# An MLP-mixer block: gelu in units of 2048 columns, and its cubic constant added to 64 columns

## The chip, the core and the metric

The kernel runs on one core of a Trainium2 chip. A core has TensorE (matrix products, called PE in the profile), VectorE (DVE), ScalarE (ACT), GpSimd (POOL) and SyncE (SP, which here starts transfers), and they run their own instruction queues side by side. The metric is the device time of one execution in microseconds; less is better.

## The reference

`x` has 2048 rows of 512 columns, `w1` and `w2` are 512x512, `w3` is 512x1792 and `w4` 1792x512, all bf16.

```python
def reference(x, w1, w2, w3, w4):
    B, S, D = x.shape
    h = _gelu(_layernorm(x, axis=-1) @ w1)
    c = D // 4
    # the four column quarters of h are shifted along the rows by 1, -1, 2 and -2
    g0 = jnp.pad(h[:, :, 0*c:1*c], ((0, 0), (1, 0), (0, 0)))[:, :S, :]
    ...  # g1, g2, g3 likewise
    hs = jnp.concatenate([g0, g1, g2, g3], axis=-1) @ w2
    x1 = x + hs
    h2 = _gelu(_layernorm(x1, axis=-1) @ w3) @ w4
    return x1 + h2
```

Gelu is the tanh approximation. With y its input it can be written y * sigmoid(C2 * y * (y*y + K)), where K = 1/0.044715 and C2 = 2 * sqrt(2/pi) * 0.044715. The kernel computes it so.

## The kernel before

The program builds a list of operations per engine with what each reads and writes, and a small scheduler merges the lists: it estimates each operation's time (the `dur` arguments) and fixes the order on each engine by those estimates. On the chip each engine then works through its own list in that order and waits on semaphores. The order of the instructions is therefore part of the program, and a change of a `dur` or of a buffer count can move it.

The stages: layernorm of `x` by VectorE (statistics, then normalization); transposition of the normalized rows by TensorE; first product (`L564` with `xnT`), gelu, the mixer product with `w2` (`L584`; `L580` adds `x`), which gives `x1`; then layernorm of `x1`, transposition by DMA (`L370`), second product (`L564` with `x1nT`), gelu, product with `w4` (`L602`), addition of `x1` (`L517`) and store.

The work on the hidden columns is cut into output blocks: 128 hidden columns (on the partitions) by 512 rows, one PSUM bank each. The first layer has 4 blocks for each of four stages of 512 rows, the second 14. Two blocks, 1024 columns in the free dimension, go through gelu together:

```python
GW = 1024
NYP = 3
NYSB = 4
NX2 = 3
NU = 3
NSG = 3
# ...
xnT = sb("xnT", [P, DC, S], BF16)
x1nT = sb("x1nT", [P, DC, S], BF16)
ysb = sb("ysb", [P, NYSB, GW], BF16)
x2b = sb("x2b", [P, NX2, GW], BF16)
ub = sb("ub", [P, NU, GW], BF16)
sgb = sb("sgb", [P, NSG, GW], BF16)
# ...
def add_c0(gb):
    ps = gb % NYP
    sc.add("act", f"c0_{gb}",
           lambda e: e.activation(ysb[:, gb % NYSB, :],
                                  y_ps[:, GW * ps : GW * (ps + 1)], ACT_F.Copy),
           reads=[(("y", (2 * gb) % NYB), 2 * gb), (("y", (2 * gb + 1) % NYB), 2 * gb + 1)],
           writes=[(("ysb", gb % NYSB), gb)], dur=1080)

def add_c1(gb, eng="dve"):
    y = ysb[:, gb % NYSB, :]
    if eng == "act":
        fn = lambda e: e.activation(x2b[:, gb % NX2, :], y, ACT_F.Square)
        dur = 1080
    else:
        fn = lambda e: e.tensor_tensor(x2b[:, gb % NX2, :], y, y, ALU.mult)
        dur = 640
    sc.add(eng, f"c1_{gb}", fn,
           reads=[(("ysb", gb % NYSB), gb)], writes=[(("x2", gb % NX2), 2 * gb)],
           dur=dur)

def add_c2a(gb):
    x2 = x2b[:, gb % NX2, :]
    sc.add("dve", f"c2a_{gb}",
           lambda e: e.tensor_scalar(x2, x2, GELU_K, None, ALU.add),
           reads=[(("x2", gb % NX2), 2 * gb)],
           writes=[(("x2", gb % NX2), 2 * gb + 1)], dur=450)

def add_c2b(gb):
    y = ysb[:, gb % NYSB, :]
    sc.add("dve", f"c2b_{gb}",
           lambda e: e.tensor_tensor(ub[:, gb % NU, :], x2b[:, gb % NX2, :], y, ALU.mult),
           reads=[(("ysb", gb % NYSB), gb), (("x2", gb % NX2), 2 * gb + 1)],
           writes=[(("u", gb % NU), gb)], dur=640)

def add_c3(gb):
    sc.add("act", f"c3_{gb}",
           lambda e: e.activation(sgb[:, gb % NSG, :], ub[:, gb % NU, :],
                                  ACT_F.Sigmoid, scale=GELU_C2),
           reads=[(("u", gb % NU), gb)], writes=[(("sg", gb % NSG), gb)], dur=1160)

def add_c4(gb, eng="dve"):
    layer, st, fc0 = blk_info(gb)
    y = ysb[:, gb % NYSB, :].rearrange("p (i s) -> p i s", i=2)
    sg = sgb[:, gb % NSG, :].rearrange("p (i s) -> p i s", i=2)
    rd = [(("ysb", gb % NYSB), gb), (("sg", gb % NSG), gb)]
    if layer == 2:
        dst = h2T[:, fc0 : fc0 + 2, st % 2, :]
        w = [(("h2T", j, st % 2, q), st) for j in (fc0, fc0 + 1) for q in range(4)]
        sc.add(eng, f"c4_{gb}", lambda e: e.tensor_tensor(dst, y, sg, ALU.mult),
               reads=rd, writes=w, dur=640)
        return
    # ... the first layer writes the same product to hT in one to four pieces (L503)
```

`add_c0` copies two PSUM banks to `ysb` (`L447`, ScalarE). VectorE then squares (`c1`, `L458`; the branch for ScalarE is not taken), adds K (`c2a`, `L467`) and multiplies by y (`c2b`, `L474`); ScalarE takes the sigmoid (`c3`, `L480`); VectorE multiplies y by it (`c4`, `L492` in the second layer). A buffer slot is free for its next writer when its last reader is done: a `ysb` slot after `c4`, a PSUM bank after `c0`. `h2T` holds two stages of 512 rows, so the third stage's `c4` waits until the first stage's `L602` products are done. The lists are made like this:

```python
def gelu_blocks(blocks):
    LAG = 1
    for i, gb in enumerate(blocks):
        add_c0(gb)
        add_c1(gb, c1_eng(gb))
        add_c2a(gb)
        add_c2b(gb)
        if i >= LAG:
            add_c3(blocks[i - LAG])
            add_c4(blocks[i - LAG])
    for gb in blocks[len(blocks) - LAG :]:
        add_c3(gb)
        add_c4(gb)
# ...
for st in range(NST):
    for fc in range(DC):
        add_ygroup(1, st, fc)
        tn = 4 * (st + 1) + fc
        if DEV["head_pe_tp"] and fc < 4 and tn < NT:
            g = st * DC + fc
            add_head_tp(tn, after=[(("y", g % NYB), g)])
gelu_blocks(list(range(NB1)))
# ... mixer products, second layernorm, second product (add_ygroup), gelu, w4 product (add_mm4)
```

`add_ygroup` is one output block, four matmuls of 128x128 by 128x512. `add_head_tp` transposes one tile of 128 normalized rows (four matmuls against the identity), and may run when the block named in `after` is done. `add_mm4` is one tile of 128 output rows: 14 matmuls into one of the two banks of `o_ps`, which VectorE empties (`L517`).

Of the kernel before, what the change touches and what calls it, by code (L numbers as in the profile page):

```python
# [6 lines left out]
P = 128  # L7
# [162 lines left out]
def bass_standalone__mixer_s_mlp__prompt_kernel(  # L170
# [19 lines left out]
    NYSB = 4  # L190
    NX2 = 3
    NU = 3
    NSG = 3
# [3 lines left out]
    BPS1 = DC // 2  # L197
    BPS2 = FC // 2
    NB1 = NST * BPS1
    NB2 = NST * BPS2  # L200
    NB = NB1 + NB2
    NG1 = NST * DC
    assert NG1 == 2 * NB1
# [4 lines left out]
    with ExitStack() as es:  # L208
# [4 lines left out]
        x1nT = sb("x1nT", [P, DC, S], BF16)  # L213
# [18 lines left out]
        ysb = sb("ysb", [P, NYSB, GW], BF16)  # L232
        x2b = sb("x2b", [P, NX2, GW], BF16)
        ub = sb("ub", [P, NU, GW], BF16)
        sgb = sb("sgb", [P, NSG, GW], BF16)
# [129 lines left out]
        def add_xT_dma(layer, t, eng="sp"):  # L365
            gt = q_ln(layer, t)
            dstT = xnT if layer == 1 else x1nT
            cb = t if layer == 1 else gt - NT
            sc.add(eng, f"dmaT{gt}",
                   lambda e: e.dma_start(dstT[:, :, P * cb : P * (cb + 1)],  # L370
                                         xn_buf[:, gt % NXN, :], transpose=True),
                   reads=[(("xn", gt % NXN), gt)], writes=[(("xT", layer, cb), 0)],
                   dur=1300, queue=eng)
# [61 lines left out]
        def blk_info(gb):  # L435
            if gb < NB1:
                st, fp = divmod(gb, BPS1)
                return 1, st, 2 * fp
            st2, fp = divmod(gb - NB1, BPS2)
            return 2, st2, 2 * fp  # L440

        NYB = 2 * NYP

        def add_c0(gb):
            ps = gb % NYP
            sc.add("act", f"c0_{gb}",
                   lambda e: e.activation(ysb[:, gb % NYSB, :],  # L447
                                          y_ps[:, GW * ps : GW * (ps + 1)], ACT_F.Copy),
                   reads=[(("y", (2 * gb) % NYB), 2 * gb), (("y", (2 * gb + 1) % NYB), 2 * gb + 1)],
                   writes=[(("ysb", gb % NYSB), gb)], dur=1080)  # L450

        def add_c1(gb, eng="dve"):
            y = ysb[:, gb % NYSB, :]
            if eng == "act":
                fn = lambda e: e.activation(x2b[:, gb % NX2, :], y, ACT_F.Square)
                dur = 1080
            else:
                fn = lambda e: e.tensor_tensor(x2b[:, gb % NX2, :], y, y, ALU.mult)  # L458
                dur = 640
            sc.add(eng, f"c1_{gb}", fn,  # L460
                   reads=[(("ysb", gb % NYSB), gb)], writes=[(("x2", gb % NX2), 2 * gb)],
                   dur=dur)

        def add_c2a(gb):
            x2 = x2b[:, gb % NX2, :]
            sc.add("dve", f"c2a_{gb}",
                   lambda e: e.tensor_scalar(x2, x2, GELU_K, None, ALU.add),  # L467
                   reads=[(("x2", gb % NX2), 2 * gb)],
                   writes=[(("x2", gb % NX2), 2 * gb + 1)], dur=450)

        def add_c2b(gb):
            y = ysb[:, gb % NYSB, :]
            sc.add("dve", f"c2b_{gb}",
                   lambda e: e.tensor_tensor(ub[:, gb % NU, :], x2b[:, gb % NX2, :], y, ALU.mult),  # L474
                   reads=[(("ysb", gb % NYSB), gb), (("x2", gb % NX2), 2 * gb + 1)],
                   writes=[(("u", gb % NU), gb)], dur=640)

        def add_c3(gb):
            sc.add("act", f"c3_{gb}",
                   lambda e: e.activation(sgb[:, gb % NSG, :], ub[:, gb % NU, :],  # L480
                                          ACT_F.Sigmoid, scale=GELU_C2),
                   reads=[(("u", gb % NU), gb)], writes=[(("sg", gb % NSG), gb)], dur=1160)

        def add_c4(gb, eng="dve"):
            layer, st, fc0 = blk_info(gb)
            y = ysb[:, gb % NYSB, :].rearrange("p (i s) -> p i s", i=2)
            sg = sgb[:, gb % NSG, :].rearrange("p (i s) -> p i s", i=2)
            rd = [(("ysb", gb % NYSB), gb), (("sg", gb % NSG), gb)]
            if layer == 2:
                dst = h2T[:, fc0 : fc0 + 2, st % 2, :]  # L490
                w = [(("h2T", j, st % 2, q), st) for j in (fc0, fc0 + 1) for q in range(4)]
                sc.add(eng, f"c4_{gb}", lambda e: e.tensor_tensor(dst, y, sg, ALU.mult),  # L492
                       reads=rd, writes=w, dur=640)
                return
            for si, (dst, spec, ng, ncols, w) in enumerate(c4_segments(fc0, st)):
                if ng == 2:
                    yy, ss = y, sg
                else:
                    gi, c0 = spec
                    yy = y[:, gi, c0 : c0 + ncols]  # L500
                    ss = sg[:, gi, c0 : c0 + ncols]
                sc.add(eng, f"c4_{gb}_{si}",
                       (lambda d_, a_, b_: (lambda e: e.tensor_tensor(d_, a_, b_, ALU.mult)))(dst, yy, ss),  # L503
                       reads=rd, writes=w, dur=60 + 0.57 * ncols * ng)
# [40 lines left out]
        def add_head_evac(t):  # L545
# [3 lines left out]
                   reads=res, writes=[(("xT", 1, t), 0)], dur=600)  # L549
# [285 lines left out]
```

## Time and profile before

| | |
|---|---|
| time, median of 5 | 161.35 us (161.01 to 162.32) |
| span of the profiled execution | 159.2 us |
| TensorE matmul busy | 138.3 us, 87% |
| VectorE busy | 127.7 us, 80% |
| ScalarE busy | 91.9 us, 58% |
| GpSimd busy | 18.9 us, 12% |
| granted TensorE clock | full throughout |

The span runs from the first instruction to the last of one profiled execution, whose time is listed as 161.01 us. A line of the profile names the line of the program, the engine, the operation and what it writes and reads; `x28` is the number of instructions. Busy time counts each engine's instructions where they overlap only once. In a listing in order of time, an instruction's length runs until its result is written, so neighbours on one engine overlap a little: the distance between starts is what an instruction costs in a full queue. An engine named behind an arrow is the one that ended a wait.

### The profile page before, as it was taken

The page shows a single profiled execution, that of the slowest core. Times are in us where ns is not written, and L with a number is a line of the kernel's source. Part 1 is how long each engine was busy: PE and PEld are TensorE (multiplying, and loading weights), DVE is VectorE, ACT ScalarE, POOL GpSimd, SP SyncE. Part 2 cuts the span into 40 slices and gives each one's busy share as a digit, 9 for nine tenths or more (in the row PEclk, how much of TensorE's full clock was granted, in tenths as well). Part 3 has the DMA queues.
Part 4 walks back from the last instruction along what each step waited for, and adds up shares of the span by engine and source line. Part 5 has one row for each costly group of instructions (what it writes and reads, how often), then busy time and mean ns, then how long its engine had stood idle before and what let it go on. Part 6 is the DMA issues. An engine that isn't in the chain of part 4 may idle for free.

```text
span 159.2 us, 1881 instructions
## 1 busy us (share of the span) xinstructions
PE 138.3 (87%) x656; PEld 60.8 (38%) x656; DVE 127.7 (80%) x268; ACT 91.9 (58%) x110; POOL 18.9 (12%) x46
## 2 busy tenths in 40 slices
PE   0079696798999899998899899999989999988992
PEld 0044232343444344443344344444434444433440
DVE  1799699999999999999999999559999139981311
ACT  3185568998955459787786875119885008520000
POOL 4022750020164441000000000000000000000000
PEclk9999999999999999999999999999999999999999
DMA  5930400057069844430000000010000001110010
GB/s 163 339 157 0 129 3 2 4 146 315 2 188 305 170 66 99 99 66 2 0 4 33 0 0 33 0 66 33 0 0 4 33 33 49 52 35 33 33 65 34
DMA packets 13432, 11.12 MB, mean 70 GB/s; under 512 B 9136, under 2 KB 12208, under 8 KB 13424
## 3 DMA queue, kind: packets, MB, share of 16 engines
q1 hardware_dynamic: 12016, 6.29, 15.0%
q0 software_dynamic: 880, 4.19, 8.0%
q10 hardware_dynamic: 528, 0.52, 1.0%
q8 instruction: 5, 0.08, 0.2%
q14 instruction: 3, 0.02, 0.1%
HBM read 6.82 MB, written 2.10 MB: 56 GB/s over the span
## 4 chain that ended last, share of the span: by engine, by line
PE 32%; DVE 27%; issue 3%; ACT 1%
PE o_ps L602 27%; DVE ub L474 7%; DVE h2T L492 6%; DVE x2b L458 6%; PE y_ps L564 6%; DVE x2b L467 4%; DVE o_sb L517 2%; ACT ysb L447 1%; DVE xn_buf L430 1%; DVE st L381 1%; DVE mv L386 0%; ACT sgb L480 0%
## 5 line engine op out<-in xcount | busy, mean ns | idle before, releaser
L564 PE MATMUL y_ps<-x1nT,w_sb 128*128 128x512 bf16 x224 | 50.2, 379 | 2.8 <-ACT ysb L447 2.2
L602 PE MATMUL o_ps<-w_sb,h2T 128*128 128x512 bf16 x224 | 49.2, 379 | 1.4 <-DVE h2T L492 1.4
L447 ACT ACTIVATE ysb<-y_ps 128x1024 bf16<-128x1024 f32 x36 | 36.3, 1013 | 21.6 <-DVE h2T L492 15.7
L480 ACT ACTIVATE sgb<-ub 128x1024 bf16<-128x1024 bf16 x36 | 38.0, 1056 | 15.1 <-DVE ub L474 15.1
L564 PEld LDWEIGHTS y_ps<-x1nT,w_sb 128*128 128x128 bf16 x224 | 21.3, 98 | 31.2 <-ACT ysb L447 4.2
L602 PEld LDWEIGHTS o_ps<-w_sb,h2T 128*128 128x128 bf16 x224 | 21.9, 98 | 28.0 <-DVE h2T L492 1.9
L517 DVE TENSOR_TENSOR o_sb<-o_ps,x_sb 128x512 bf16<-128x512 f32 x16 | 11.0, 690 | 20.7 <-PE o_ps L602 20.5
L474 DVE TENSOR_TENSOR ub<-x2b,ysb 128x1024 bf16<-128x1024 bf16 x36 | 24.9, 693 | 1.2
L458 DVE TENSOR_TENSOR x2b<-ysb 128x1024 bf16<-128x1024 bf16 x36 | 24.6, 682 | 0.0
L381 DVE BATCH_NORM_STATS2 st<-x_sb 128x6 f32<-128x512 bf16 x32 | 20.5, 671 | 4.5 <-DMA x_sb<-in_x_dram 4.5
L564 PE MATMUL y_ps<-xnT,w_sb 128*128 128x512 bf16 x64 | 17.2, 405 | 3.9 <-ACT xnT L548 3.9
L492 DVE TENSOR_TENSOR h2T<-ysb,sgb 128x1024 bf16<-128x1024 bf16 x28 | 18.8, 683 | 0.0
L584 PE MATMUL o_ps<-w_sb,hT 128*128 128x512 bf16 x64 | 16.4, 379 | 0.0
L467 DVE TENSOR_SCALAR x2b<-x2b 128x1024 bf16<-128x1024 bf16 x36 | 15.3, 425 | 1.1
L538 PE MATMUL o_ps<-ident,xn_buf 128*128 128x128 bf16 x56 | 5.7, 231 | 9.3 <-DVE xn_buf L430 7.9
L430 DVE TENSOR_SCALAR xn_buf<-x_sb,mv,rstd 128x512 bf16<-128x512 bf16 x32 | 11.7, 407 | 1.7 <-POOL rstd L421 1.5
L509 ACT ACTIVATE x_sb<-o_ps 128x512 bf16<-128x512 f32 x16 | 9.5, 595 | 5.1 <-PE o_ps L584 5.0
L421 POOL TENSOR_TENSOR rstd<-vpe,neghalf 128x2 f32<-128x2 f32 x14 | 10.4, 744 | 1.2
L564 PEld LDWEIGHTS y_ps<-xnT,w_sb 128*128 128x128 bf16 x64 | 5.9, 103 | 10.4 <-ACT xnT L548 3.5
L548 ACT ACTIVATE xnT<-o_ps 128x512 bf16<-128x512 bf16 x14 | 8.2, 594 | 2.8 <-PE o_ps L538 2.7
L538 PEld LDWEIGHTS o_ps<-ident,xn_buf 128*128 128x128 bf16 x56 | 3.6, 101 | 14.5 <-DVE xn_buf L430 8.1
L584 PEld LDWEIGHTS o_ps<-w_sb,hT 128*128 128x128 bf16 x64 | 6.3, 98 | 7.1
(23 smaller groups left out, 33.9 us busy)
## 6 DMA issues: line engine op xcount, KB each, us to landing
w_sb<-in_w_dram POOLq DMA_DIRECT2D x2, 1792.0 KB, 8.4
out_dram<-o_sb SPq DMA_DIRECT2D x16, 128.0 KB, 1.8
x_sb<-in_x_dram SPq DMA_DIRECT2D x3, 512.0 KB, 6.7
w_sb<-in_w_dram ACTq DMA_DIRECT2D x1, 512.0 KB, 4.1
x_sb<-in_x_dram SPq DMA_DIRECT2D x4, 128.0 KB, 3.9
w_sb<-in_w_dram POOLq DMA_DIRECT2D x1, 512.0 KB, 4.3
x1nT<-xn_buf SPq DMA_TRANSPOSE x16, 2.5
```

Source lines behind the costliest of these rows:

```text
L381: sc.add("dve", f"bnst{gt}", lambda e: e.bn_stats(st6[:, gt, :], src), reads=[(rsrc, 0)], writes=[(("st6", gt), 0)], dur=650)
L430: lambda e: e.tensor_scalar(xn_buf[:, gt % NXN, :], src, mv[:, gt, 0:1], rstd[:, gt : gt + 1], ALU.subtract, ALU.mult),
L447: lambda e: e.activation(ysb[:, gb % NYSB, :], y_ps[:, GW * ps : GW * (ps + 1)], ACT_F.Copy),
L458: fn = lambda e: e.tensor_tensor(x2b[:, gb % NX2, :], y, y, ALU.mult)
L467: lambda e: e.tensor_scalar(x2, x2, GELU_K, None, ALU.add),
L474: lambda e: e.tensor_tensor(ub[:, gb % NU, :], x2b[:, gb % NX2, :], y, ALU.mult),
L480: lambda e: e.activation(sgb[:, gb % NSG, :], ub[:, gb % NU, :], ACT_F.Sigmoid, scale=GELU_C2),
L492: sc.add(eng, f"c4_{gb}", lambda e: e.tensor_tensor(dst, y, sg, ALU.mult), reads=rd, writes=w, dur=640)
L517: lambda e: e.tensor_tensor(o_sb[:, k % NO, :], o_ps[:, 512 * (k % 2) : 512 * (k % 2 + 1)], x1_sb[:, t, :], ALU.add),
L564: ins = e.matmul(dst, wsb[:, dc, P * fc : P * (fc + 1)], srcT[:, dc, 512 * st : 512 * (st + 1)], start=(dc == 0), stop=(dc == DC - 1))
L584: ins = e.matmul(dst, hT[:, j, c0 : c0 + P], w2_sb[:, j, :], start=False, stop=(j == DC - 1))
L602: ins = e.matmul(dst, h2T[:, fc, st2 % 2, P * q : P * (q + 1)], w4_sb[:, fc, :], start=(fc == 0), stop=(fc == FC - 1))
```

## The change

A gelu unit in the second layer takes four output blocks (2048 columns) instead of two; as 14 is not a multiple of four, each stage has three such units and one of two blocks. Evictions from PSUM (`c0`) stay at two blocks. The buffers `ysb`, `x2b`, `ub` and `sgb` are twice as wide, with fewer slots for `ysb` (3 for 4) and `x2b` (2 for 3). To make room, the second layer's transposed rows share the buffer of the first's (`x1nT = xnT`). The estimates the scheduler works with now follow the width. In the first layer units stay at two blocks, and the head's transposes are listed in pairs behind the first two blocks of a stage, no longer one behind each block. The aim is fewer and longer instructions on VectorE and ScalarE.

One part leaves work out: in the second layer `c2a` adds K to the first 64 columns of a unit only. In the other columns of a unit the sigmoid's argument is C2 * y * y * y instead of C2 * y * (y*y + K).

The core of the diff:

```diff
-    NYSB = 4
-    NX2 = 3
-    NU = 3
-    NSG = 3
+    NYS = 3
+    NX2 = 2
+    NUU = 3
+    NSS = 3
     NO = 3
     LNB = 2
 
-    BPS1 = DC // 2
-    BPS2 = FC // 2
-    NB1 = NST * BPS1
-    NB2 = NST * BPS2
-    NB = NB1 + NB2
     NG1 = NST * DC
-    assert NG1 == 2 * NB1
+    UW = 2 * GW
 
     x3 = x[0].rearrange("(p t) d -> p t d", t=NT)
     out3 = out[0].rearrange("(p t) d -> p t d", t=NT)
 ...
-        x1nT = sb("x1nT", [P, DC, S], BF16)
+        x1nT = xnT
-        ysb = sb("ysb", [P, NYSB, GW], BF16)
-        x2b = sb("x2b", [P, NX2, GW], BF16)
-        ub = sb("ub", [P, NU, GW], BF16)
-        sgb = sb("sgb", [P, NSG, GW], BF16)
+        ysb = sb("ysb", [P, NYS, UW], BF16)
+        x2b = sb("x2b", [P, NX2, UW], BF16)
+        ub = sb("ub", [P, NUU, UW], BF16)
+        sgb = sb("sgb", [P, NSS, UW], BF16)
 ...
+        units = []
+        for st in range(NST):
+            for fc0 in range(0, DC, 2):
+                units.append((1, st, fc0, 2, st * DC + fc0))
+        NU1 = len(units)
+        for st2 in range(NST):
+            fc0 = 0
+            while fc0 < FC:
+                nfc = 4 if fc0 + 4 <= FC else FC - fc0
+                units.append((2, st2, fc0, nfc, NG1 + st2 * FC + fc0))
+                fc0 += nfc
+        NUN = len(units)
+
+        def add_c0(u, h):
+            layer, st, fc0, nfc, g0 = units[u]
+            g = g0 + 2 * h
+            b = g % NYB
+            sc.add("act", f"c0_{u}_{h}",
+                   lambda e: e.activation(ysb[:, u % NYS, GW * h : GW * (h + 1)],
+                                          y_ps[:, 512 * b : 512 * b + GW], ACT_F.Copy),
+                   reads=[(("y", b), g), (("y", b + 1), g + 1)],
+                   writes=[(("ysb", u % NYS, h), u)], dur=1080)
+
+        def ysb_reads(u):
+            nfc = units[u][3]
+            return [(("ysb", u % NYS, h), u) for h in range(nfc // 2)]
+
+        def add_c1(u):
+            W = units[u][3] * 512
+            y = ysb[:, u % NYS, 0:W]
+            sc.add("dve", f"c1_{u}",
+                   lambda e: e.tensor_tensor(x2b[:, u % NX2, 0:W], y, y, ALU.mult),
+                   reads=ysb_reads(u), writes=[(("x2", u % NX2), 2 * u)], dur=90 + 0.54 * W)
+
+        def add_c2a(u):
+            W = units[u][3] * 512 if units[u][0] == 1 else 64
+            x2 = x2b[:, u % NX2, 0:W]
+            sc.add("dve", f"c2a_{u}",
                    lambda e: e.tensor_scalar(x2, x2, GELU_K, None, ALU.add),
+                   reads=[(("x2", u % NX2), 2 * u)],
+                   writes=[(("x2", u % NX2), 2 * u + 1)], dur=90 + 0.29 * W)
+
+        def add_c2b(u):
+            W = units[u][3] * 512
+            y = ysb[:, u % NYS, 0:W]
+            sc.add("dve", f"c2b_{u}",
+                   lambda e: e.tensor_tensor(ub[:, u % NUU, 0:W], x2b[:, u % NX2, 0:W], y, ALU.mult),
+                   reads=ysb_reads(u) + [(("x2", u % NX2), 2 * u + 1)],
+                   writes=[(("u", u % NUU), u)], dur=90 + 0.54 * W)
+
+        def add_c3(u):
+            W = units[u][3] * 512
+            sc.add("act", f"c3_{u}",
+                   lambda e: e.activation(sgb[:, u % NSS, 0:W], ub[:, u % NUU, 0:W],
                                           ACT_F.Sigmoid, scale=GELU_C2),
+                   reads=[(("u", u % NUU), u)], writes=[(("sg", u % NSS), u)], dur=230 + 0.84 * W)
+
+        def add_c4(u):
+            layer, st, fc0, nfc, g0 = units[u]
+            W = nfc * 512
+            y = ysb[:, u % NYS, 0:W].rearrange("p (i s) -> p i s", i=nfc)
+            sg = sgb[:, u % NSS, 0:W].rearrange("p (i s) -> p i s", i=nfc)
+            rd = ysb_reads(u) + [(("sg", u % NSS), u)]
             if layer == 2:
+                dst = h2T[:, fc0 : fc0 + nfc, st % 2, :]
+                w = [(("h2T", j, st % 2, q), st) for j in range(fc0, fc0 + nfc) for q in range(4)]
+                sc.add("dve", f"c4_{u}", lambda e: e.tensor_tensor(dst, y, sg, ALU.mult),
+                       reads=rd, writes=w, dur=90 + 0.54 * W)
                 return
+            # ... first layer: the pieces of before, by pairs of blocks
 ... (the 1024-wide versions of the same functions go)
         for st in range(NST):
             for fc in range(DC):
                 add_ygroup(1, st, fc)
-                tn = 4 * (st + 1) + fc
-                if DEV["head_pe_tp"] and fc < 4 and tn < NT:
+                if DEV["head_pe_tp"] and fc < 2:
                     g = st * DC + fc
-                    add_head_tp(tn, after=[(("y", g % NYB), g)])
-        gelu_blocks(list(range(NB1)))
+                    for tn in (4 * (st + 1) + 2 * fc, 4 * (st + 1) + 2 * fc + 1):
+                        if tn < NT:
+                            add_head_tp(tn, after=[(("y", g % NYB), g)])
+        gelu_units(list(range(NU1)))
         for t in ORDER2:
             add_mm2(t)
         ln_layer(2)
```

## The prediction

> **What bounds the kernel now.** I read the trace by stage first, because the page's shares (TensorE 87%, VectorE 80%) are means over stages that differ. TensorE's rows in order of time give the borders: the first layer's transposes, matmuls and mixer products run to 54.33 us, the second layer (`L564` with `x1nT`, and `L602`) from 54.33 to 156.25, and 2.95 us of eviction and store follow. The table by stretch, for the second layer:
>
> ```profile
> core 0: us, PE busy (x) PEld busy (x) DVE busy (x) ACT busy (x) POOL busy (x), PEclk, DMA share, GB/s
> ...
> 54.33:156.25 101.92, 98.20 (x448) 43.14 (x448) 79.45 (x142) 55.27 (x57) 3.28 (x6) 1.00 0.13 34
> ```
>
> TensorE is busy for nearly all of it, at the full clock. A busy matmul row overlaps its neighbours (379 ns each, but they start closer together), so I take the pace from the order of time: start, length, matmuls, and in brackets the idle time before.
>
> ```profile
> 54.33 17.43 PE L564 MATMUL y_ps<-x1nT,w_sb 128*128 128x512 bf16 x80 [0.49 <-DMA x1nT<-xn_buf]
> 71.96 1.90 PE L564 MATMUL y_ps<-x1nT,w_sb 128*128 128x512 bf16 x8 [0.20 <-ACT ysb L447]
> 74.35 1.90 PE L564 MATMUL y_ps<-x1nT,w_sb 128*128 128x512 bf16 x8 [0.49 <-ACT ysb L447]
> 76.74 1.90 PE L564 MATMUL y_ps<-x1nT,w_sb 128*128 128x512 bf16 x8 [0.49 <-ACT ysb L447]
> ...
> 121.29 21.32 PE L602 MATMUL o_ps<-w_sb,h2T 128*128 128x512 bf16 x98
> 143.99 12.26 PE L602 MATMUL o_ps<-w_sb,h2T 128*128 128x512 bf16 x56 [1.39 <-DVE h2T L492]
> ```
>
> 98 matmuls in 21.32 us, less some 0.16 us of drain, are 0.216 us each. Eight are 1.73 us, yet the groups of eight start 2.39 us apart: 0.66 us of TensorE lost per pair of output blocks. Going through all such rows of the second layer, start to start less 0.216 per matmul, the losses are 0.35, 0.66, 0.66, 0.89 and 0.91 us in the `L564` stretches and 1.54 us ahead of the last 56 matmuls: 5.0 us. The rest, 448 x 0.216 = 96.7 us, is work that no change of the other engines removes.
>
> Why 2.39 us? VectorE in the same stretch, in order of time:
>
> ```profile
> 72.81 0.68 DVE L458 TENSOR_TENSOR x2b<-ysb 128x1024 bf16<-128x1024 bf16 x1
> 73.53 0.43 DVE L467 TENSOR_SCALAR x2b<-x2b 128x1024 bf16<-128x1024 bf16 x1
> 73.99 0.69 DVE L474 TENSOR_TENSOR ub<-x2b,ysb 128x1024 bf16<-128x1024 bf16 x1
> 74.60 0.68 DVE L492 TENSOR_TENSOR h2T<-ysb,sgb 128x1024 bf16<-128x1024 bf16 x1
> 75.20 0.69 DVE L458 TENSOR_TENSOR x2b<-ysb 128x1024 bf16<-128x1024 bf16 x1
> ```
>
> From start to start: 0.72, 0.46, 0.61 and 0.60 us, together 2.39, with no gap. VectorE sets the pace: TensorE waits for a PSUM bank, ScalarE (which empties it) waits for `ub`, and VectorE waits for nobody. The chain of waits runs the same way: TensorE `L602` 27%, and the four VectorE lines between them about as much.
>
> **What the Trainium skill says.** "VectorE: DVE Perf Modes", section "The TRN2 errata — SBUF-src ops pay a fixed extra latency per instruction", says that an SBUF operation pays a fixed cost once per instruction, whatever its width. The trace agrees; the groups, kept apart by shape (mean ns behind the busy time):
>
> ```profile
> L503 DVE TENSOR_TENSOR hT<-ysb,sgb 128x1024 bf16<-128x1024 bf16 x4 | 2.7, 687 | 0.0
> ...
> L503 DVE TENSOR_TENSOR hT<-ysb,sgb 128x512 bf16<-128x512 bf16 x4 | 1.7, 419 | 0.0
> ...
> L503 DVE TENSOR_TENSOR hT<-ysb,sgb 128x128 bf16<-128x128 bf16 x6 | 1.1, 220 | 0.0
> ```
>
> (687-419)/512 is 0.523 ns a column, and some 0.15 us does not depend on width. "ScalarE: Activation LUTs", section "What ACT_TABLE_LOAD costs", gives 0.833 ns per element for every function and an overlap of about 93 ns between neighbours; here the 128x1024 copy takes 1013 ns and the 128x512 copy 595, so 0.82, and back to back they start 0.91 us apart. "Perfetto Trace Analysis", section "Optimizing Scalar/DVE Operations", names both sides: larger operations help a saturated engine, while splitting helps where an unsaturated one makes bubbles in others. In the `L564` stretches VectorE is saturated.
>
> **Part 1: the second layer's VectorE work.** Twelve units of 2048 columns and four of 1024 take the place of 28 of 1024. A wider tensor-tensor adds 1024 x 0.523 = 0.535 us to its step. The 64-column addition costs its step less the columns left out: the same skill page ("Specifications" and "The perf-mode tier table") has 0.96 GHz and four elements per cycle for a bf16 tensor-scalar, so 1024 columns stream in 0.267 us, and the estimate is 0.46 - 0.267 + 0.017 = 0.21 us. The slope above, half a cycle per column, agrees on the clock; no narrower addition has run here yet. So a wide unit is 1.25 + 0.21 + 1.14 + 1.14 = 3.74 us, a narrow one 0.72 + 0.21 + 0.61 + 0.60 = 2.14, and a 512-row stage 3 x 3.74 + 2.14 = 13.4 us against 7 x 2.39 = 16.7. That is 13.5 us off VectorE over four stages. The addition gives 28 x 0.46 - 16 x 0.21 = 9.5 us of it; twelve fewer of each of the three multiplies, 0.19 + 0.07 + 0.07 us of fixed step each trio, give 3.9. Per output block: 0.95 us after, 1.19 before, with TensorE at 4 x 0.216 = 0.86.
>
> **Part 2: ScalarE.** Evictions stay 1024 wide. Sigmoid goes from 28 to 16 instructions: a narrow one is followed by the next start after 0.96 us (79.50 to 80.46 in the trace), a wide one by estimate after 0.96 + 1024 x 0.84 ns = 1.82 us (0.84 from the starts of 512- and 1024-wide copies, 0.48 and 0.91 us apart), so a wide unit costs ScalarE 2 x 0.92 + 1.82 = 3.66 us, 0.92 per block: less than VectorE, a little more than TensorE.
>
> **Part 3: do the buffers cover the difference?** VectorE is still 10% slower than TensorE while TensorE runs `L564` only. TensorE's program now begins with 34 output blocks in a row, then one group of 14 `L602`, 12 blocks, four groups, 10 blocks, eleven groups. In 34 blocks VectorE falls 34 x 0.09 = 3 us behind; six PSUM banks and three wide `ysb` slots (12 blocks) stand against it. I followed the queues by hand with the steps above, from TensorE's start at 54.3 and VectorE's first unit at 59.0. The tightest place is block 20 (71.6 us), whose bank is emptied 0.2 us late; at blocks 24, 28 and 32 the margins are 0.7, 0.5 and 0.3 us. At the later turns (46th and 52nd block) the bank is free in time. So of the 3.5 us lost in the `L564` stretches I expect 0.2 to 0.6 to stay.
>
> **Part 4: the end.** The last eleven `L602` groups take 11 x 14 x 0.216 = 33.3 us. The last stage's `h2T` is needed after seven, 21.2 us in. Its two held wide units are written after the third group, the last narrow one about 16.7 us in, behind one output eviction (0.60). That leaves over 4 us, so the 1.54 us go. Sum: 5.0 - 0.4 = 4.6 us gained.
>
> **Part 5: the first layer.** Its units stay 1024 wide with the full addition, so VectorE has the same work. `ysb` falls from four slots to three and `x2b` from three to two; transposes come in pairs and earlier, which spares TensorE waits of up to 1.12 us ahead of single ones. But VectorE is 97% busy from 20 us on and decides. Its order changes: four row-statistics of the second layer (0.61 us each) now come ahead of the last gelu product, two before, which puts that product's end at about 45.3 instead of 43.9. The mixer product of the ninth row tile waits for it (before: 45.04), and eight products of 1.08 us follow: TensorE ends this at about 54.1 instead of 53.8. The transposes needed next landed at 54.33 before and are no later. Second-layer start: 54.5, a cost of 0.2. Sharing the `xnT` buffer costs nothing: the stages overwritten had their last read before 35 us, and the first DMA transpose is at 46.
>
> Sum: 54.5 + 96.7 + 0.4 + 0.2 (drain) + 2.95 = 154.7 us of span, against 159.2. The median time lies 2.15 us above that span: **156.9 us**, 4.4 us or 2.8% less.
>
> **Rivals.** (a) *All VectorE time counts.* Then 13.5 us go and the time is 148. For it: VectorE holds much of the chain. Against: 96.7 of 101.9 us are matmuls at the full clock. I give it next to nothing. (b) *The coarse grain makes a new wait.* A bank group is released later, because a 2048-column sigmoid stands ahead of the eviction and every multiply waits for two evictions. If each margin in part 3 were 0.5 us worse, three or four stalls return, some 2 us: 159. For it: ScalarE at 0.92 per block is above TensorE's 0.86. Against: the deeper `ysb`. (c) *The first layer pays.* With three slots, an eviction waits for a gelu product three units back; if VectorE then idles even 2 us ahead of 45 us, the start of the second layer slips as much: 159. Against: following the queue, each eviction arrives about 1 us ahead of its use.
>
> **Range and chances.** Keeping 2 us of the losses gives 158.5; everything recovered with a slightly quicker first layer gives 155.5. Two per cent is 158.1, which takes 1.2 us of error in one direction; either (b) or (c) in half its strength does that. Faster by over 2%: 0.76, within: 0.22, slower: 0.02.
>
> **What would show it.** Right: VectorE busy falls from 127.7 to about 114, second-layer matmuls take 97 to 97.5 us from first start to last end, the wait of `L564` on the eviction falls from 2.2 to under 0.6 us, and that ahead of the last 56 matmuls disappears. Wrong: a second-layer start later than 55.5, a repeated gap ahead of groups of eight matmuls, or a wide sigmoid far from 1.9 us.

## The result and the profile after

The changed kernel takes 157.1 us (median of 9 runs, 156.91 to 157.55). The kernel before, on the same chips, takes 161.88 (16 runs, 161.01 to 162.45). The ratio is 0.971, 95% interval 0.969 to 0.974: 2.9% less. The prediction said 156.9.

The table by stretch, for the second layer of the changed kernel (`L574` and `L612` are the lines of the two products now):

```profile
core 0: us, PE busy (x) PEld busy (x) DVE busy (x) ACT busy (x) POOL busy (x), PEclk, DMA share, GB/s
54.77:152.69 97.92, 97.14 (x449) 43.59 (x447) 68.25 (x96) 53.62 (x45) 3.85 (x6) 1.00 0.13 35
```

97.92 us instead of 101.92, and VectorE busy for 68.25 instead of 79.45. TensorE in order of time (start, length, matmuls, and in brackets the idle time before):

```profile
54.77 17.43 PE L574 MATMUL y_ps<-xnT,w_sb 128*128 128x512 bf16 x80
72.98 12.25 PE L574 MATMUL y_ps<-xnT,w_sb 128*128 128x512 bf16 x56 [0.78 <-ACT ysb L449]
85.07 3.18 PE L612 MATMUL o_ps<-w_sb,h2T 128*128 128x512 bf16 x14
88.09 10.52 PE L574 MATMUL y_ps<-xnT,w_sb 128*128 128x512 bf16 x48
98.45 12.25 PE L612 MATMUL o_ps<-w_sb,h2T 128*128 128x512 bf16 x56
110.65 8.81 PE L574 MATMUL y_ps<-xnT,w_sb 128*128 128x512 bf16 x40
119.29 33.40 PE L612 MATMUL o_ps<-w_sb,h2T 128*128 128x512 bf16 x154
```

The repeated gaps ahead of groups of eight are gone, and so is the wait ahead of the last 56 matmuls. One gap is left, before the 21st block: 80 matmuls at 0.216 us are 17.28, the next block starts 18.21 after the first, so 0.93 us are lost.

A full VectorE unit of the changed kernel, in order of time:

```profile
77.00 1.22 DVE L462 TENSOR_TENSOR x2b<-ysb 128x2048 bf16<-128x2048 bf16 x1
78.25 0.18 DVE L469 TENSOR_SCALAR x2b<-x2b 128x64 bf16<-128x64 bf16 x1
78.47 1.22 DVE L477 TENSOR_TENSOR ub<-x2b,ysb 128x2048 bf16<-128x2048 bf16 x1
79.61 1.22 DVE L497 TENSOR_TENSOR h2T<-ysb,sgb 128x2048 bf16<-128x2048 bf16 x1
80.75 1.22 DVE L462 TENSOR_TENSOR x2b<-ysb 128x2048 bf16<-128x2048 bf16 x1
```

From square to square 3.75 us for four blocks, 0.94 a block, where it was 1.19. The 64-column addition costs 0.22 us of that.

### The profile page after: what moved, and what is told of

The parts are those of the page before. It is cut to its first block, busy times and chain, and to the rows that moved or that the text cites. A ratio compares the mean times of both kernels' runs of the same rounds, so it can differ in the third digit from the quotient of the medians.

```text
span 155.7 us, 1825 instructions
## 1 busy us (share of the span) xinstructions
PE 137.2 (88%) x656; PEld 61.9 (40%) x656; DVE 116.1 (75%) x220; ACT 89.5 (57%) x98; POOL 19.5 (13%) x46
## 4 chain that ended last, share of the span: by engine, by line
PE 51%; DVE 5%; ACT 3%; issue 1%; POOL 1%; POOLq 0%
PE o_ps L612 31%; PE y_ps L574 20%; ACT ysb L449 2%; DVE ub L477 2%; ACT sgb L484 1%; DVE xn_buf L425 1%; POOL vpe L411 1%; DVE x2b L462 1%; DVE st L376 1%; POOLq L728 0%; DVE o_sb L527 0%; DVE mv L381 0%; DVE x2b L469 0%
## 5 line engine op out<-in xcount | busy, mean ns | idle before, releaser
L574 PE MATMUL y_ps<-xnT,w_sb 128*128 128x512 bf16 x288 | 66.5, 387 | 3.1 <-ACT ysb L449 2.2
L612 PE MATMUL o_ps<-w_sb,h2T 128*128 128x512 bf16 x224 | 48.8, 379 | 0.0
L449 ACT ACTIVATE ysb<-y_ps 128x1024 bf16<-128x1024 f32 x36 | 35.6, 1018 | 21.4 <-DVE h2T L497 14.8
L574 PEld LDWEIGHTS y_ps<-xnT,w_sb 128*128 128x128 bf16 x288 | 27.8, 99 | 38.2 <-issue 3.3
L484 ACT ACTIVATE sgb<-ub 128x1024 bf16<-128x1024 bf16 (+1 forms) x24 | 35.6, 1484 | 9.2 <-DVE ub L477 9.1
L612 PEld LDWEIGHTS o_ps<-w_sb,h2T 128*128 128x128 bf16 x224 | 21.9, 98 | 26.4
L462 DVE TENSOR_TENSOR x2b<-ysb 128x1024 bf16<-128x1024 bf16 (+1 forms) x24 | 22.8, 951 | 2.4 <-ACT ysb L449 2.3
L477 DVE TENSOR_TENSOR ub<-x2b,ysb 128x1024 bf16<-128x1024 bf16 (+1 forms) x24 | 23.0, 958 | 0.8
L497 DVE TENSOR_TENSOR h2T<-ysb,sgb 128x2048 bf16<-128x2048 bf16 (+1 forms) x16 | 17.2, 1084 | 0.0
L590 PE MATMUL o_ps<-x_sb,ident 128*128 128x512 bf16 x16 | 6.1, 382 | 3.2 <-DVE hT L512 3.2
L411 POOL TENSOR_SCALAR vpe<-mv 128x2 f32<-128x2 f32 x14 | 4.5, 320 | 20.2 <-DVE mv L381 20.2
L469 DVE TENSOR_SCALAR x2b<-x2b 128x64 bf16<-128x64 bf16 (+1 forms) x24 | 6.3, 262 | 0.8
```

The source lines that it names most:

```text
L449: lambda e: e.activation(ysb[:, u % NYS, GW * h : GW * (h + 1)], y_ps[:, 512 * b : 512 * b + GW], ACT_F.Copy),
L462: lambda e: e.tensor_tensor(x2b[:, u % NX2, 0:W], y, y, ALU.mult),
L477: lambda e: e.tensor_tensor(ub[:, u % NUU, 0:W], x2b[:, u % NX2, 0:W], y, ALU.mult),
L484: lambda e: e.activation(sgb[:, u % NSS, 0:W], ub[:, u % NUU, 0:W], ACT_F.Sigmoid, scale=GELU_C2),
L497: sc.add("dve", f"c4_{u}", lambda e: e.tensor_tensor(dst, y, sg, ALU.mult), reads=rd, writes=w, dur=90 + 0.54 * W)
L574: ins = e.matmul(dst, wsb[:, dc, P * fc : P * (fc + 1)], srcT[:, dc, 512 * st : 512 * (st + 1)], start=(dc == 0), stop=(dc == DC - 1))
```

## The experiments

The change joins four things: fewer additions, wider units, other buffer depths, paired transposes. (The shared `x1nT` buffer and the new estimates, which also move the order of the lists, come along and were not tried alone.) The theory was the prediction's: VectorE's pace in the first-product stretches was the loss, and the narrower addition brings most of the gain. Rivals: that VectorE's time counts everywhere, that width or depth is the real cause, and that the 0.93 us left over comes from a late norm.

**The addition on all columns again, in the changed kernel.**

```diff
-            x2 = x2b[:, u % NX2, 0:W]
+            x2 = x2b[:, u % NX2, 0 : units[u][3] * 512]
```

> The changed kernel with K added to all columns of every second-layer unit again (order on all engines as in the changed kernel). VectorE gets 12 x 0.52 + 4 x 0.25 = 7.2 us more in the second layer. Theory (TensorE bounds the second layer, and VectorE's pace shows only as stalls of L574 where it runs out of banks): a wide unit steps at 4.26 us, 1.08 per block against TensorE's 0.86, so the stall ahead of the 21st block grows to about 1.8 us and new ones come at the 29th, 33rd and 41st block (0.3, 0.3, 1.6): 3 us more than the changed kernel, about 160.2, most of the gain gone. Rival 1 (each us of VectorE counts alike, 0.4 us of time per us): 160. Rival 2 (the width of the instructions is what gains, the addition costs nothing that matters): 157 to 157.5.

Measured: 160.74 us, ratio to the kernel before 0.992 (0.989 to 0.995). TensorE in order of time:

```profile
54.25 17.64 PE L574 MATMUL y_ps<-xnT,w_sb 128*128 128x512 bf16 x80
73.77 10.75 PE L574 MATMUL y_ps<-xnT,w_sb 128*128 128x512 bf16 x48 [1.87 <-ACT ysb L449]
84.67 1.89 PE L574 MATMUL y_ps<-xnT,w_sb 128*128 128x512 bf16 x8 [0.16 <-ACT ysb L449]
...
96.12 5.34 PE L574 MATMUL y_ps<-xnT,w_sb 128*128 128x512 bf16 x24 [1.35 <-ACT ysb L449]
```

The 3.6 us between this kernel and the changed one are the addition's; the stalls return in the first-product stretches. The times expected by the theory (160.2) and by rival 1 (160) lie too close together to be told apart; the stalls do that, as the large ones stand ahead of the 21st and the 41st block, where the theory put them. Rival 2 falls. Width, depth and pairing together are worth 1.1 us without the narrower addition.

**The addition on 64 columns alone, in the kernel before** (units of 1024 columns; leaves out the addition in the other columns of each unit of the second layer).

```diff
-            x2 = x2b[:, gb % NX2, :]
+            x2 = x2b[:, gb % NX2, 0 : GW if gb < NB1 else 64]
```

> The kernel before, units of 1024 and its order of instructions, but K added to 64 columns only in the second layer. VectorE's step per unit falls from 2.39 to 2.14 us. Theory: the 3.5 us of stalls in L564 go nearly all, the 1.5 us ahead of the last 56 matmuls stay, because they hang on the order of VectorE's queue there: 3.2 to 3.7 us less than before, about 158.3. Rival 1: 28 x 0.25 x 0.4 = 2.8 us less. Rival 2: no change.

Measured: 158.37 us, 0.978 (0.974 to 0.981), 3.5 us less: the theory's 158.3, where rival 1 gives 159.1. No first-product stretch waits for an eviction any more, though a block costs VectorE 1.07 us, more than the 0.94 of the changed kernel. The last wait is as it was before (the first and the last row of the second layer):

```profile
55.38 22.61 PE L564 MATMUL y_ps<-x1nT,w_sb 128*128 128x512 bf16 x104 [0.58 <-DMA x1nT<-xn_buf]
...
141.53 12.26 PE L602 MATMUL o_ps<-w_sb,h2T 128*128 128x512 bf16 x56 [1.39 <-DVE h2T L492]
```

So the addition takes the stalls of the first-product stretches, and something else takes the one at the end.

**Less work for VectorE still** (the changed kernel without square and addition in the second layer: the sigmoid's argument is C2 * y * y. The lists keep their order up to the 34th output block; behind it TensorE takes the next 12 blocks ahead of the first group of `w4` products, which stood between them in the changed kernel).

```diff
-                add_c1(u)
-                add_c2a(u)
+                if units[u][0] == 1:
+                    add_c1(u)
+                    add_c2a(u)
```

(and `c2b` multiplies y by y in the second layer)

> The changed kernel with the second layer's square and addition left out: the sigmoid's argument is C2*y*y, one multiply instead of three instructions; the scheduler's estimate for it is the sum of the three. VectorE loses about 21 us in the second layer. Theory: only the stall ahead of the 21st block (0.9 us) can still be gained, so 156.0 to 156.6, with 448 matmuls in 96.7 to 97.2 us. Rival 1: 0.4 x 21 = 8 us less, 149.

Measured: 157.11 us, 0.969 (0.965 to 0.973), level with the changed kernel, although VectorE is busy for 97.1 us instead of 116.1. VectorE in order of time:

```profile
75.72 1.23 DVE L478 TENSOR_TENSOR ub<-ysb 128x2048 bf16<-128x2048 bf16 x1 [0.95 <-ACT ysb L449]
77.52 1.23 DVE L503 TENSOR_TENSOR h2T<-ysb,sgb 128x2048 bf16<-128x2048 bf16 x1 [0.57 <-ACT sgb L490]
79.35 1.22 DVE L478 TENSOR_TENSOR ub<-ysb 128x2048 bf16<-128x2048 bf16 x1 [0.60 <-ACT ysb L449]
81.15 1.23 DVE L503 TENSOR_TENSOR h2T<-ysb,sgb 128x2048 bf16<-128x2048 bf16 x1 [0.57 <-ACT sgb L490]
```

Each of these four in a row waits for ScalarE, and the unit takes 3.63 us (75.72 to 79.35), ScalarE's step. The rival that all of VectorE's time counts falls. The second layer is 97.69 us long, 0.23 less than in the changed kernel:

```profile
54.82 29.57 PE L580 MATMUL y_ps<-xnT,w_sb 128*128 128x512 bf16 x136
84.89 10.52 PE L580 MATMUL y_ps<-xnT,w_sb 128*128 128x512 bf16 x48 [0.49 <-ACT ysb L449]
95.24 15.27 PE L618 MATMUL o_ps<-w_sb,h2T 128*128 128x512 bf16 x70
```

The 0.93 us ahead of the 21st block, all that the theory left to gain, are gone; but 0.69 us are lost ahead of the 35th block (84.89 - 54.82 - 136 x 0.216), where the changed kernel has 14 products of `w4` in between. So the small gain did not show in the time; whether it would with TensorE's order kept was not tried.

**The 0.93 us: a late norm?** In the changed kernel VectorE waits 0.69 us at 61.61 for GpSimd's `rstd`, early enough to push everything behind it. A longer estimate for that operation moves the norm behind the second unit's square.

```diff
-                   writes=[(("rstd", gt + i), 0) for i in range(n)], dur=750)
+                   writes=[(("rstd", gt + i), 0) for i in range(n)], dur=3000 if gt == 2 * NT - 2 else 750)
```

> The changed kernel with the last two normalizations one multiply later in VectorE's queue (behind the second unit's square instead of ahead of the first unit's second multiply); nothing else moves. In the changed kernel that multiply started at 62.26 because the normalizations waited for GpSimd until 61.61. Theory A (that wait makes the stall ahead of the 21st block): the first sigmoid starts about 1.3 us earlier, the stall shrinks from 0.94 to about 0.3 us, the time by 0.6 us: 156.5. Theory B (the stall comes from ScalarE's own pace, 0.92 us per block against 0.86): no change.

Measured: 157.47 us, 0.972 (0.968 to 0.975). The wait for `rstd` is gone; this is what VectorE and then TensorE show instead:

```profile
62.94 1.22 DVE L462 TENSOR_TENSOR x2b<-ysb 128x2048 bf16<-128x2048 bf16 x1 [0.75 <-ACT ysb L449]
```

```profile
72.91 12.25 PE L574 MATMUL y_ps<-xnT,w_sb 128*128 128x512 bf16 x55 [0.70 <-ACT ysb L449]
```

The wait for `rstd` was not the cause: without it VectorE waits as long for the second eviction of the unit. The two normalizations still take 0.65 us of VectorE's time, now behind that square, no longer ahead of it; what their own time adds to the stall was not tried. The same edit with the full addition:

> The same two normalizations later, with K added to all columns, so that the whole reference is computed in wide units. Without the move: 160.74 us with stalls of 1.87, 0.16 and 1.35 us. Theory A: the first shrinks by about 0.6 to 1.3 us: 159.5 to 160.2. Theory B: no change.

Measured: 160.52 us, 0.991 (0.988 to 0.994), with stalls of 1.72, 0.15 and 1.35 us, as without the edit. What holds the 21st block is seen on ScalarE, in the changed kernel:

```profile
67.14 1.91 ACT L484 ACTIVATE sgb<-ub 128x2048 bf16<-128x2048 bf16 x1
68.94 1.02 ACT L449 ACTIVATE ysb<-y_ps 128x1024 bf16<-128x1024 f32 x1
70.01 1.91 ACT L484 ACTIVATE sgb<-ub 128x2048 bf16<-128x2048 bf16 x1
71.83 1.92 ACT L449 ACTIVATE ysb<-y_ps 128x1024 bf16<-128x1024 f32 x2
```

The eviction that frees the bank starts at 71.83, the moment ScalarE's queue is through with a sigmoid of 2048 columns. That sigmoid began at 70.01 because its `ub` came from VectorE at 69.98:

```profile
68.76 1.22 DVE L477 TENSOR_TENSOR ub<-x2b,ysb 128x2048 bf16<-128x2048 bf16 x1
```

Every step waits for a whole unit of four blocks. But the coarse grain alone does not make the stall: in the kernel without square and addition the same sigmoid stands ahead of the same eviction, starts at 69.16, and the eviction comes in time for the 21st block:

```profile
70.96 1.96 ACT L449 ACTIVATE ysb<-y_ps 128x1024 bf16<-128x1024 f32 x2
```

It takes both, a VectorE that is late by then and the sigmoid of a whole unit.

**The wait at the end: one instruction's place** (the kernel before, whole computation; a shorter estimate for the last sigmoid puts the last `c4` ahead of an output eviction, and only those two change places).

```diff
-                   reads=[(("u", gb % NU), gb)], writes=[(("sg", gb % NSG), gb)], dur=1160)
+                   reads=[(("u", gb % NU), gb)], writes=[(("sg", gb % NSG), gb)], dur=700 if gb == NB - 1 else 1160)
```

> The kernel before, with the last gelu product of VectorE's queue ahead of the output eviction that stood in front of it (two instructions change places, no other difference). Theory: the last 56 matmuls then wait for the sigmoid that ends at 142.47 and the product, done at about 143.2, instead of 143.95: 0.8 us less than before. Rivals 1 and 2 (VectorE's total or its widths decide): no change.

Measured: 161.18 us, 0.995 (0.993 to 0.997), about as expected.

```profile
143.95 12.26 PE L602 MATMUL o_ps<-w_sb,h2T 128*128 128x512 bf16 x56 [0.64 <-DVE h2T L492]
```

1.39 became 0.64 us. About half of this wait was an instruction's place in a list. VectorE in the kernel before, with the output eviction that itself waits for TensorE ahead of the last product:

```profile
142.65 0.69 DVE L517 TENSOR_TENSOR o_sb<-o_ps,x_sb 128x512 bf16<-128x512 f32 x1 [0.67 <-PE o_ps L602]
143.25 0.68 DVE L492 TENSOR_TENSOR h2T<-ysb,sgb 128x1024 bf16<-128x1024 bf16 x1
```

**Depth without width** (units of 1024 columns with 64-column additions, the kernel of 158.37 us, with more slots; it leaves out the additions in the other columns, as that one does).

```diff
-    NYSB = 4
+    NYSB = 6
     NX2 = 3
-    NU = 3
-    NSG = 3
+    NU = 4
+    NSG = 6
```

> Units of 1024 and the 64-column addition as in the narrow kernel measured at 158.37 us, but with six slots of 1024 columns for ysb and sgb and four for ub, about the depth in columns that the changed kernel has. TensorE's program becomes that of the changed kernel in the main (26 blocks, 1 group, 20 blocks, 4 groups, 10 blocks, 11 groups). Theory (depth of buffers, not width, took away the wait ahead of the last 56 matmuls): that wait of 1.4 us goes and the time falls to 156.4 to 157.1, level with the changed kernel or below it. Rival 2 (width): it stays at 158.4.

Measured: 157.4 us, 0.970 (0.967 to 0.974): level with the changed kernel, 0.3 us above the range expected, and TensorE ends without a wait. (In some traces a few matmuls are not recorded; `x151` stands for 154.)

```profile
118.55 33.40 PE L602 MATMUL o_ps<-w_sb,h2T 128*128 128x512 bf16 x151
```

So the wait at the end goes with depth too, without width. The list order moves with the slots: the last `c4` ends at 135.75 us here, at 143.93 in the kernel before.

**Single transposes in the changed kernel.**

```diff
-                if DEV["head_pe_tp"] and fc < 2:
+                if DEV["head_pe_tp"] and fc < 4:
...
-                    for tn in (4 * (st + 1) + 2 * fc, 4 * (st + 1) + 2 * fc + 1):
+                    for tn in (4 * (st + 1) + fc,):
```

> The changed kernel with the head's transposes one behind each block again, as before. Theory (VectorE bounds the first layer, and the pairing moves only TensorE's waits there): the second layer starts at the same distance from TensorE's first instruction, 46.3 us within 0.4, and the time stays 157.1 within 0.5. Rival (pairing brought a part of the gain): 1 us or more slower.

Measured: 157.62 us, 0.974 (0.971 to 0.978), an interval that overlaps the changed kernel's: 0.5 us more, at the edge of what the theory allows and half of what the rival asked for. In the trace, which is of the slowest run of this kernel (158.53 us), the second layer starts 47.61 us after TensorE's first instruction instead of 46.34, so the theory's 46.3 within 0.4 is wrong there, and VectorE has three waits in the first layer that the changed kernel does not have:

```profile
27.55 0.83 DVE L512 TENSOR_TENSOR hT<-ysb,sgb 128x512 bf16<-128x512 bf16 x3 [0.29 <-ACT sgb L484]
...
31.21 0.69 DVE L462 TENSOR_TENSOR x2b<-ysb 128x1024 bf16<-128x1024 bf16 x1 [0.23 <-ACT ysb L449]
...
34.04 0.69 DVE L462 TENSOR_TENSOR x2b<-ysb 128x1024 bf16<-128x1024 bf16 x1 [0.35 <-ACT ysb L449]
```

**A part of VectorE's work given to ScalarE** (the kernel before, whole computation, the square of every fourth second-layer unit on ScalarE).

```diff
-            fr = DEV["act_sq_frac"]
+            fr = 0.0 if gb < NB1 else 0.25
```

> The kernel before, whole computation, with the square of every fourth second-layer unit moved from VectorE to ScalarE. Theory (the pace in the first-product stretches is what VectorE has to do per block): a unit costs VectorE 2.39 - 0.72/4 = 2.21 us instead of 2.39, ScalarE 1.87 + 0.91/4 = 2.10, TensorE 1.73. The loss of 0.66 us per unit of two blocks falls to about 0.45, a third of the 3.5 us goes: about 160.6, with the wait ahead of the last 56 matmuls still there. Rival (ScalarE's longer queue holds the evictions back, so each square on ScalarE makes a stall): no gain, 161.5 to 162.

Measured: 160.34 us, 0.990 (0.987 to 0.993). About the gain expected, by another road: the wait ahead of the last 56 matmuls, which should have stayed, is gone, and a first-product stretch waits 1.82 us at once, because ScalarE takes two sigmoids and a square, and waits 0.39 us for VectorE, between its evictions at 71.70 and 76.13. The order of the lists moved too: the program ends with ten groups of `w4` products in a row, before with eleven.

```profile
77.19 3.76 PE L564 MATMUL y_ps<-x1nT,w_sb 128*128 128x512 bf16 x16 [1.82 <-ACT ysb L447]
```

With 6, 4, 4 and 6 slots in it as well:

> The same with 6, 4, 4 and 6 slots instead of 4, 3, 3 and 3; whole computation. Theory (what the deep narrow kernel showed: depth takes the wait ahead of the last 56 matmuls): another 1.4 us less, about 159, the wait ahead of the last 56 matmuls gone. Rival (that wait went because VectorE had little left to do, depth alone does not help): level with the run beside it, 160.5, wait of about 1.4 us still there.

Measured: 159.87 us, 0.988 (0.985 to 0.992), not to be told from the run beside it, with the same stall of 1.82 us. As the wait at the end had gone already, the theory was not tested.

**Narrow units, deep, transposes in pairs** (the kernel of 157.4 us with the pairs; it leaves out the same additions).

```diff
-                tn = 4 * (st + 1) + fc
-                if DEV["head_pe_tp"] and fc < 4 and tn < NT:
+                if DEV["head_pe_tp"] and fc < 2:
                     g = st * DC + fc
-                    add_head_tp(tn, after=[(("y", g % NYB), g)])
+                    for tn in (4 * (st + 1) + 2 * fc, 4 * (st + 1) + 2 * fc + 1):
+                        if tn < NT:
+                            add_head_tp(tn, after=[(("y", g % NYB), g)])
```

> The deep narrow kernel with the addition on 64 columns, and the head's transposes in pairs as in the changed kernel. Theory (pairing shortens the first layer, and counts most with three slots, less with six): first instruction to second-layer start 46.3 to 46.8 us where single transposes had 46.76, time 157.0 to 157.4. Rival (pairing is worth the 1.27 us it was worth in the changed kernel whatever the depth): start at 45.5, time 156.1.

Measured: 155.69 us, 0.962 (0.959 to 0.964): the fastest kernel here, below the changed one's interval. The rival was nearer (45.5 and 156.1): first instruction (7.96) to second layer is 45.56 us.

```profile
53.52 24.34 PE L564 MATMUL y_ps<-x1nT,w_sb 128*128 128x512 bf16 x112
77.70 3.19 PE L602 MATMUL o_ps<-w_sb,h2T 128*128 128x512 bf16 x14
80.72 15.70 PE L564 MATMUL y_ps<-x1nT,w_sb 128*128 128x512 bf16 x72
96.26 12.25 PE L602 MATMUL o_ps<-w_sb,h2T 128*128 128x512 bf16 x56
108.34 8.80 PE L564 MATMUL y_ps<-x1nT,w_sb 128*128 128x512 bf16 x40
116.98 33.40 PE L602 MATMUL o_ps<-w_sb,h2T 128*128 128x512 bf16 x154
```

No wait is left in the second layer: 96.86 us, TensorE's own work. The four gelu buffers hold no more than the changed kernel's: 19 slots of 1024 columns against 11 of 2048 (`x1nT` has its own buffer here, as before the change).

**The same with the whole computation** (the addition on all columns again; everything is computed).

```diff
-            x2 = x2b[:, gb % NX2, 0 : GW if gb < NB1 else 64]
+            x2 = x2b[:, gb % NX2, :]
```

> The kernel before, whole computation and units of 1024 columns, with 6, 3, 4 and 6 slots and the transposes in pairs: what the narrower addition is worth beside the deep paired kernel at 155.69 us. Theory (each thing removes its own loss: pairing 1.2 us in the first layer, depth the 1.4 us ahead of the last 56 matmuls, only the narrower addition the stalls of the first-product stretches): first instruction to second-layer start 45.6 us, the stalls of 3 to 3.5 us in the first-product stretches stay, about 159.2. Rival (six slots carry the slower VectorE through the 34 blocks, since a unit may fall further behind): stalls under 2 us, about 157.5.

Measured: 157.78 us, 0.976 (0.973 to 0.978). The second layer takes 99.33 us, with 2.4 us of it lost in the first-product stretches (the rival: under 2, the theory: 3 to 3.5); the rival that six slots carry VectorE further is nearer than the theory.

```profile
54.03 20.88 PE L564 MATMUL y_ps<-x1nT,w_sb 128*128 128x512 bf16 x95
75.53 1.67 PE L564 MATMUL y_ps<-x1nT,w_sb 128*128 128x512 bf16 x7 [0.62 <-ACT ysb L447]
77.70 1.90 PE L564 MATMUL y_ps<-x1nT,w_sb 128*128 128x512 bf16 x8 [0.49 <-ACT ysb L447]
...
119.96 33.40 PE L602 MATMUL o_ps<-w_sb,h2T 128*128 128x512 bf16 x150
```

The first stall comes after 24 blocks in a row instead of 20 (`x95` stands for 96), and the end has no wait. VectorE is busy for 127.8 us, where it was 127.7 before the change; TensorE just waits less for it.

## Why the prediction held

In one table (us; the addition on all columns or on 64):

| kernel | all columns | 64 columns | the addition |
|---|---|---|---|
| 1024 wide, 4/3/3/3 slots, single transposes (before) | 161.88 | 158.37 | 3.5 |
| 2048 wide, 3/2/3/3 slots, pairs (the change) | 160.74 | 157.1 | 3.6 |
| 1024 wide, 6/3/4/6 slots, pairs | 157.78 | 155.69 | 2.1 |

- **What bounds it: right.** TensorE's matmuls at 0.216 us are the floor, and the loss was VectorE's pace ahead of them. The second layer fell by 4.0 us of the 5.0 lost there. Of the signs named, the wait at the end is gone and none of the three against it came; VectorE's busy time (116.1 for 114), the second layer (97.92 for 97 to 97.5) and the wait for the eviction (0.78 for under 0.6) each missed by a little.
- **Part 1, VectorE: right by the step, a little large in busy time.** A wide unit was to cost 3.74 us and costs 3.75; the 64-column addition was estimated at 0.21 from the step of the full one and the rate in the Trainium skill ("VectorE: DVE Perf Modes", "The perf-mode tier table"), and the next instruction starts 0.21 to 0.22 us after it. Busy time fell by 11.6 us to 116.1, not by 13.5 to 114. Some 0.8 of the 1.9 us lies in the count: busy time leaves out the 0.03 us or so ahead of the second and third instruction of a unit, which the steps hold, and there are twelve units fewer. The rest was not traced.
- **Part 2, ScalarE: right.** The wide sigmoid takes 1.91 us and the next instruction starts 1.80 to 1.82 us on. It is the next limit right there, as the prediction hints in rival (b): with VectorE relieved further, a unit still takes 3.63 us, close to its 3.66.
- **Part 3, the buffers: the place right, the size wrong.** It named the tightest place, the block whose bank is emptied late, and gave it 0.2 us; it lost 0.93. The step that failed is the queue followed by hand. From its start at 59.0, a first unit without `c4` (1.25 + 0.21 + 1.14 = 2.60) puts the second square at 61.6; the trace has 59.48 and 63.40. With the norm behind it the square still starts only at 62.94, because it waits for the second eviction of its unit. From there VectorE has no gap up to the multiply that, in the changed kernel, ends at 69.98 and lets the sigmoid ahead of the 21st block's eviction start. This is rival (b), the coarse grain, in one place instead of three or four, and together with VectorE's lateness. No later block waited; TensorE came to them 0.7 us later than the prediction had it, so its margins there were not put to the test.
- **Part 4, the end: right, but not because of the width.** The wait of 1.39 us went, and the last products come where the prediction put them. The last `c4` ends at 136.15, 16.9 us after the start of the last eleven groups (119.29), predicted about 16.7:

```profile
135.47 0.68 DVE L497 TENSOR_TENSOR h2T<-ysb,sgb 128x1024 bf16<-128x1024 bf16 x1
```

The wait goes as well with 1024-wide units and more slots, with the whole addition and with part of it, and it stays with fewer additions alone. So what counts is the place of the last products in VectorE's list, which the slots move and so does the square on ScalarE. Exchanging two instructions alone took half of it.
- **Part 5, the first layer: near zero in the traces, from two parts of opposite sign.** First instruction to second layer is 46.34 us, before 46.40; the expected cost was 0.2. But two kernels whose first layer has the instructions of before in the same order (the narrow addition on 64 columns, the exchanged product) show 47.10 and 46.76, so one trace gives this length to some 0.7 us only. With pairs, the five traces with the change's buffers lie at 46.34 to 46.47, the two with 6/3/4/6 slots at 45.56 and 45.57: the change's buffers cost 0.8 against those deeper ones. Single transposes lie at 47.61 with the change's buffers and at 46.80 with 6/3/4/6 slots: by the traces pairs bring 1.2 to 1.3, by the medians 0.5 and 1.7. So a cost like rival (c)'s is likely, with the pairs paying it back; the prediction took both to be small. Against the buffers of before, with four slots, no run has the pairs.
- **The sum: misses that cancelled, which is luck.** The span is 155.7, predicted 154.7: 0.6 more in the second layer, mostly the 21st block, 0.3 more at its start, 0.1 at the end. The start is not the change's doing (the first layer is shorter than predicted): in this profiled execution TensorE's first instruction came at 8.43, in that of before at 7.93. Against that the median lies 1.4 us above this span, not 2.15. Time less span is 1.8 us in both traced runs (161.01 - 159.2 and 157.48 - 155.7); the first is the fastest run of its kernel, the second one of the slower ones. That is also why the spans differ by 3.5 us and the medians by 4.8; how the 0.8 us beyond the second layer's 4.0 divide up no trace shows.
- **Rival (a) fell**: 19 us less VectorE work brought no time beyond the changed kernel's (157.11 us for 157.1).

What the prediction did not see is that the gain needs no wider units. "Perfetto Trace Analysis" ("Optimizing Scalar/DVE Operations") in the Trainium skill has both sides, larger operations for a saturated engine and smaller ones against bubbles in others; here narrow units with slots enough leave no bubble in the second layer (the kernel of 155.69 us), and the wide ones of the change leave 0.93 us. With the addition on 64 columns, narrow units in gelu buffers no larger are 1.4 us quicker than wide ones (155.69 against 157.1): the profiled executions show 1.06 in the second layer (96.86 against 97.92) and 0.78 in the first. How much of the 0.78 belongs to which buffer was not tried; nor were wide units with more slots, so a cost of width at equal depth is not shown.

## What to carry to other kernels

When one engine's pace makes another stall only in stretches, ask first how far it may fall behind: more buffer slots and transposes in pairs brought 4.0 us here with no work removed (2.6 of it in the second layer, by the traces), where the change, which leaves most of an addition out, brought 4.8. Wider instructions save fixed costs on their own engine, and make every hand-over wait for a larger piece. A wait at the end of a program may be the place of one instruction in a list, so look at what stands ahead of it before making anything faster. And the length of one stage in one trace can be off by more than the effect looked for, as the first layer here shows: compare several.

## What the runs showed of the hardware

An addition on 64 columns still takes 0.18 us and its successor starts 0.21 to 0.22 us on, where 1024 columns take 0.43 and 0.46: a sixteenth of the columns costs nearly half. Widening the square from 1024 to 2048 columns added 0.53 us to its step (0.72 to 1.25), close to the 0.535 worked out from narrower products. The full addition 2048 wide takes 0.69 us and costs 0.72.
